# Window attention and two dense layers: the 64-token tiles of two batches as one unit

## Chip, core and metric

One core of a Trainium2 chip. The metric is the device time of one execution in microseconds (us).

## What is computed

Causal attention with a window of 128 keys and a linear bias per head (4 batches, 8 heads, 576 tokens, head dimension 64), then two dense layers in float32 on the 2304 tokens. Cut to what matters here:

```python
scores = scale * np.matmul(q, k.transpose(0, 1, 3, 2))
mask = (rel >= 0) & (rel < window)          # rel = query - key, window = 128
attn = softmax(np.where(mask, scores + bias[None], -1e9))
x = np.matmul(attn, v)                      # 4 x 8 x 576 x 64
x = x.transpose(0, 2, 1, 3).reshape(2304, 512)
x = silu(x @ w_in) @ w_out                  # 512 -> 2048 -> 512
out = relu(x @ w2_in) ** 2 @ w2_out
```

## The kernel before, in words

A sequence of 576 tokens is four tiles of 128 tokens and one tile of 64. The 16 full tiles of the four batches make four blocks of 512 columns; the four 64-token tiles make a fifth block of 256 columns. A **unit** is one tile and one pair of heads (`units`, L85): 64 units of full tiles, and 16 **narrow** units, 80 in all.

Attention of the first 20 units runs ahead of all else. The other 60 are laid between the matmuls of the first dense layer, whose `mm1(n)` (L544) is called once in each of 64 **slots** n: 12 matmuls of 512 columns, 16 slots to a block. Eight more slots (L547 to L558) do the fifth block. Units are handled in groups of four, a group to every four slots; the table `visits` (L1019 to L1031) says in which slot a group has its scores, its transposes and its values. For the group whose first unit is u = n0 + n, scores come in slot n, transposes of the probabilities in slot n + 3, and the values (probabilities times v) in slot n + 7; where the next group is narrow, values come one slot earlier, so that in those slots there are only values, and in the next only transposes. The narrow groups have their scores in slots 44, 48, 52 and 56, their transposes in 47, 51, 55 and 59, and their values in 50, 54, 58 and 63; the values of the last full group are in slot 46.

The work of a unit: `scores` (L223) multiplies 64 queries of one head by 192 keys, once for each 64 queries and each of the two heads; the head decides which half of the array's rows is used, the half of the queries decides which columns. `maxima`, `exponentials`, `reciprocals` and `normalise` are the softmax, on VectorE, ScalarE, VectorE and GpSimd. `transpose_p` (L320) turns 64 rows of probabilities at a time, `copy_p` brings them back from PSUM, `values` (L367) or `values_of_four` (L351, for narrow groups) multiplies them by v. A narrow unit has only the first half of the queries, so half as many scores and transposes as a full one; its values have 64 columns in place of 128.

Inputs come by the DMA queue of SyncE (SP), in program order with the stores of the first layer's results (`g0d`): `load_qk` and `load_v` (L202, L210) bring q, k and v of one unit four units ahead, into places of their own, four of each. The float64 weights come as words into a place of `raw` (one place, L896) or into a spare place of the pool `w` (16 places, `spare`, L404), and are turned into float32 pairs in five steps whose slots `begin` sets (L857 to L862). The last of them, chunk (0, 1, 7), begins in slot 51 and uses `raw`.

The order of the instructions is written out by hand (`manual_schedule`): every engine runs its own in program order.

Of the kernel before, what the change touches and what calls it, by code (L numbers as in the profile page):

```python
# [8 lines left out]
F32 = mybir.dt.float32  # L9
# [7 lines left out]
P = 128  # L17
# [8 lines left out]
def kernel(  # L26
# [21 lines left out]
    nc = tc.nc  # L48
    B, NHP, S, _ = v.shape
    NT, DM = out.shape  # L50
    NF = w1.shape[0]
    D = 64
# [4 lines left out]
    raw_p = ctx.enter_context(tc.tile_pool(name="raw", bufs=1))  # L57
# [13 lines left out]
    full = [(b, t, P, min(t, P)) for b in range(B) for t in range(0, S - P + 1, P)]  # L71
    rest = [(b, S // P * P, S % P, P) for b in range(B)]
    blocks = [full[i:i + NSUB] for i in range(0, len(full), NSUB)]
    blocks.append(rest)
    NB = len(blocks)
    width = [sum(t[2] for t in tiles) for tiles in blocks]
    start = [sum(width[:j]) for j in range(NB)]
    assert sum(width) == NT and max(width) <= BLK and P % rest[0][2] == 0
    tbs = []
    for j, tiles in enumerate(blocks):  # L80
        c0 = 0
        for t in tiles:
            tbs.append((j, c0) + t)
            c0 += t[2]
    units = [t + (hp,) for t in tbs for hp in range(NHP)]  # L85
    NU = len(units)
    x_t = {}

# [6 lines left out]
    def attention(ap, ps, n0):  # L95
        slope = [2.0 ** (-8.0 * (h + 1) / H) for h in range(H)]
        xq, xk, xv, z_t, s_t, pt_t, o_t = ({} for _ in range(7))
        c = {"n0": n0}

        W = 3 * D

        def halves_of(u):

            n, m0 = units[u][4:6]
            if m0 == P:
                return [(slice(0, n), slice(0, W))]
            if u < c["n0"] and not m0:
                return [(slice(0, n), slice(D, W))]  # L110
            return [(slice(i * D, (i + 1) * D), slice(P - m0 - i * D, W)) for i in range(n // D)]

        def whole(u):

            n, m0 = units[u][4:6]
            return slice(0, n), slice(D + P - m0 - (n - D if m0 < P else 0), D + W)

        def zeros(z):
            nc.gpsimd.memset(z[..., :D], 0.0)
            nc.gpsimd.memset(z[..., D + W:], 0.0)  # L120

# [70 lines left out]
        def load_v_strip(i):  # L192
# [6 lines left out]
            for hp in range(NHP):  # L199
                xv[i * NHP + hp] = [c["va"][:, i - 1, hp] if m0 else None, c["va"][:, i, hp]]  # L200

        def load_qk(u):  # L202
            _, _, b, t0, n, m0, hp = units[u]
            if u not in xq:
                xq[u] = ap.tile([P, P], F32, tag="q", name="q", bufs=4)
                nc.sync.dma_start(out=xq[u][:, :n], in_=q[b, hp, :, t0:t0 + n])
            xk[u] = ap.tile([P, 2 * P], F32, tag="k", name="k", bufs=4)[:, P - m0:P + n]
            nc.sync.dma_start(out=xk[u], in_=k[b, hp, :, t0 - m0:t0 + n])

        def load_v(u):  # L210
            _, _, b, t0, n, m0, hp = units[u]
            t = ap.tile([P, 2, P], F32, tag="v", name="v", bufs=4)
            if m0 == n:
                nc.sync.dma_start(
                    out=t, in_=v[b, hp, t0 - m0:t0 + n, :].rearrange("(k p) d -> p k d", p=P)
                )
            else:
                if m0:
                    nc.sync.dma_start(out=t[:m0, 0], in_=v[b, hp, t0 - m0:t0, :])
                nc.sync.dma_start(out=t[:n, 1], in_=v[b, hp, t0:t0 + n, :])  # L220
            xv[u] = [t[:, 0], t[:, 1]]

        def scores(u):  # L223


            _, _, b, t0, n, m0, hp = units[u]
            lo = P - m0
            xq_, xk_ = xq.pop(u), xk.pop(u)
            apart = len(xq_.shape) == 3
            if apart:  # L230
                s = acc_p.tile([P, 2, 2 * P], F32, tag="acc", name="s")
                s = [s[:, j] for j in range(2)]
            else:
                so = c["pp" if u >= c["n0"] and u % 4 > 1 else "so"]
                s = [so[:, j, u % 2 * 2 * P:(u % 2 + 1) * 2 * P] for j in range(2)]
            if u < c["n0"] and not m0:
                for j in range(2):
                    nc.tensor.matmul(
                        s[j][:D, D:P], lhsT=c["far"], rhs=c["ident"][:, :D], start=True, stop=True
                    )  # L240
            for i in range(n // D):
                for j in range(2):
                    r = slice(i * D, (i + 1) * D)
                    first = max(lo - i * D, 0)
                    keys = slice(first + i * D - lo, W + i * D - lo)
                    h = slice(0, P) if apart else slice(j * D, (j + 1) * D)
                    nc.tensor.matmul(  # L247
                        s[j][r, first:W], lhsT=xq_[:, j, r] if apart else xq_[h, r], rhs=xk_[h, keys],
                        start=True, stop=True,
                    )  # L250
            s_t[u] = s
# [96 lines left out]
                copy(to[:n, :, 1::2], pp[:n, :, 1::2])  # L348
            pt_t[u] = pt

        def values_of_four(u):  # L351

            *_, n, m0, _ = units[u]
            pts, vts = [[t.pop(u + i) for i in range(4)] for t in (pt_t, xv)]
            o = c["o"]
            for i in range(4):
                o_t[u + i] = o[:, i - i % 2:i - i % 2 + 2]
            for kb, m in ((0, m0), (1, n)):
                for i in range(4):
                    for j in range(2):  # L360
                        nc.tensor.matmul(  # L361
                            o[j * D:(j + 1) * D, i, :n], lhsT=vts[i][kb][:m, j * D:(j + 1) * D],
                            rhs=pts[i][:m, j, kb, :n], start=kb == i == 0, stop=kb == 1,
                            skip_group_check=True,
                        )

        def values(u):  # L367
            _, _, b, t0, n, m0, hp = units[u]
            pt, vt = pt_t.pop(u), xv.pop(u)
            if u % 2 == 0:  # L370
                o = c["o"]
                if u < c["n0"] - 4 and u % 4:
                    o = c.pop("late", None) or acc_p.tile([P, 4, P], F32, tag="acc", name="o")
                first = u % 4 if u >= c["n0"] - 4 else 0
                o_t[u] = o[:, first:first + 2]
            o = o_t[u - u % 2][:, u % 2]
            for kb, m in ((0, m0), (1, n)):
                if m:
                    for j in range(2):
                        nc.tensor.matmul(  # L380
                            o[j * D:(j + 1) * D, :n], lhsT=vt[kb][:m, j * D:(j + 1) * D],
                            rhs=pt[:m, j, kb, :n], start=kb == 0 or not m0, stop=kb == 1,
                        )
# [9 lines left out]
        def x_lo(u):  # L393
            xh, xl, o = halves_of_x(u)
            nc.vector.tensor_tensor(xl, o, xh.bitcast(F32), ALU.subtract)

        return (zeros, lambda: c["z"], wake, constants, biases, load_q_apart, load_k_strip, load_v_strip, load_qk, load_v, scores, maxima, exponentials,
                reciprocals, normalise, transpose_p, copy_p, values, values_of_four, x_hi, x_lo)

# [4 lines left out]
    def spare(dtype):  # L404

        return wp.tile([P, 16 * P], F32R, tag="w", name="spare").bitcast(dtype)
# [450 lines left out]
    begin = {}  # L857
    for i in range(NI):
        begin[0, 0, i] = 2 * i - 4
        begin[0, 1, i] = 2 * NI + 5 * i  # L860
    converted = [(0, 0, i) for i in range(EARLY + 1)]
    begin[0, 0, EARLY + 1] = 1  # L862

# [35 lines left out]
    with tc.manual_schedule():  # L899
# [4 lines left out]
        n0 = ends(0) + 4  # L904
        with tc.tile_pool(name="at", bufs=2) as ap, tc.tile_pool(
            name="ps", bufs=1, space=bass.MemoryType.PSUM
        ) as ps:
            (zeros, at_z, wake, constants, biases, load_q_apart, load_k_strip, load_v_strip, load_qk, load_v, scores, maxima, exponentials,
             reciprocals, normalise, transpose_p, copy_p, values, values_of_four, x_hi, x_lo) = attention(ap, ps, n0)
            assert [t[1:4] for t in blocks[0]] == [(i * P, P, min(i, 1) * P) for i in range(NSUB)]  # L910
            load_k_strip(0, slice(0, 1))
            load_q_apart(0)
# [100 lines left out]
            def some(*us):  # L1013
                return [u for u in us if u < NU]
# [4 lines left out]
            visits = {n: [(), (), ()] for n in range((NB - 1) * NF)}  # L1019
            for n in range(4, (NB - 1) * NF, 4):  # L1020
                u = n0 + n
                narrow = u < NU and units[u][4] < P
                visits[n][2] = some(*range(u, u + 4))
                visits[n + 2 if narrow else n + 3][0] = some(*range(u - 4, u))
                visits[n + 3][1] = some(*range(u, u + 4))
            u = n0
            visits[1] = (), (u - 2, u - 1), ()
# [8 lines left out]
            left = []  # L1036
            for n in range((NB - 1) * NF):
                old, mid, new = visits[n]
                if len(old) == 4 and units[old[0]][4] < P:
                    values_of_four(old[0])  # L1040
                else:
                    for u in old:
                        values(u)
                for u in mid:
                    transpose_p(u)
                for u in new:
# [51 lines left out]
        with tc.tile_pool(name="gp", bufs=1) as gp_, tc.tile_pool(  # L1098
            name="acc2", bufs=4, space=bass.MemoryType.PSUM
# [29 lines left out]
            for i in range(4):  # L1129
                n = 4 + 10 * i  # L1130
# [9 lines left out]
            for j, x in enumerate(((1, 1, 3), (1, 1, 4))):  # L1140
                n = 18 + 10 * j
# [5 lines left out]
            for i in range(5, NI):  # L1147
                n = (29, 42, 57)[i - 5]
# [23 lines left out]
            for s in range(1, 4):  # L1172
                c = 7 * 4 * s - 21
# [57 lines left out]
            for n in range(NS):  # L1231
# [6 lines left out]
                b, fs = slots[n]  # L1238
# [22 lines left out]
            for c in range(4 * NI // 2):  # L1261
                s = 2 * c // NI
# [108 lines left out]
```

## Time and profile before

| | us |
|---|---|
| median of three runs | 869.44 (869.16 to 869.87) |
| the profiled execution, its own time | 868.8 |
| its span, first to last instruction | 867.0 |
| TensorE matmul busy | 858.0 (99%) |
| TensorE weight load busy | 764.0 (88%) |
| VectorE, ScalarE, GpSimd busy | 595.9, 461.9, 139.0 |
| granted TensorE clock, mean | 1.000 of full |

The profile is one execution. Its own time is 1.8 us over its span and 0.64 us under the median. Times in the trace are from the span's start. A busy engine is not yet one that sets the end: for that the chain of waits is read, which follows back from the last instruction what released each.

### The profile page before, as it was taken

What the parts mean: (1) busy time and instruction counts of PE and PEld (TensorE: products, weight loads), DVE (VectorE), ACT (ScalarE), POOL (GpSimd) and SP (SyncE); (2) the same over time, 40 slices, a digit from 0 to 9 for tenths busy, and PEclk for the clock granted to TensorE, in tenths of its full rate; (3) what the DMA queues carried; (4) which work ended last, traced back from release to release, by engine and by line L of the source; (5) the groups of instructions that cost most, each with busy time, mean ns of one, the idle gap of its engine ahead of it and who ended that gap; (6) DMA issues with size and microseconds to landing.
All of it is one profiled execution on the core that took longest, in us unless ns stands there. A gap on an engine that the chain in (4) does not pass through costs nothing.

```text
span 867.0 us, 17373 instructions
## 1 busy us (share of the span) xinstructions
PE 858.0 (99%) x6344; PEld 764.0 (88%) x6344; DVE 595.9 (69%) x1291; ACT 461.9 (53%) x1010; POOL 139.0 (16%) x222
## 2 busy tenths in 40 slices
PE   8999999999999999999999999999999999999998
PEld 6777888878778888888888899999999999999998
DVE  6878665656552465998646546677467789899884
ACT  8778666666563443555333456556467743434331
POOL 7788433524431000000000000000000000000000
PEclk9999999999999999999999999999999999999999
DMA  9676756766542377799875454565457954444431
GB/s 273 203 220 207 213 186 192 225 212 188 164 139 102 114 256 257 253 349 352 279 274 193 146 179 160 195 248 194 165 199 292 357 171 146 147 130 139 145 102 47
DMA packets 114613, 173.64 MB, mean 200 GB/s; under 512 B 12256, under 2 KB 73952, under 8 KB 111968
## 3 DMA queue, kind: packets, MB, share of 16 engines
q1 hardware_dynamic: 114256, 172.40, 59.8%
q8 instruction: 50, 0.82, 0.4%
q14 instruction: 35, 0.29, 0.1%
q10 hardware_dynamic: 272, 0.13, 0.1%
HBM read 111.15 MB, written 61.34 MB: 199 GB/s over the span
## 4 chain that ended last, share of the span: by engine, by line
PE 97%; ACT 1%; POOL 1%; DMA 0%; DVE 0%; issue 0%; SPq 0%; DVEq 0%; POOLq 0%; ACTq 0%
PE acc L631 23%; PE acc L790 21%; PE h L564 20%; PE a L692 12%; PE d L692 6%; PE b L692 3%; PE o L380 3%; PE h L553 3%; PE so L247 1%; PE pp L331 1%; PE s L247 1%; PE pp L247 1%; PE so L331 1%; PE o L361 1%; POOL z L300 0%; DMA spare<-in_q_dram 0%
## 5 line engine op out<-in xcount | busy, mean ns | idle before, releaser
L631 PE MATMUL acc<-g,w 128*128 128x512 f32 (+1 forms) x896 | 196.9, 382 | 0.0
L631 PEld LDWEIGHTS acc<-g,w 128*128 128x128 f32 x896 | 163.7, 188 | 33.0
L564 PE MATMUL h<-x,w 128*128 128x512 f32 x768 | 185.8, 396 | 0.0
L790 PE MATMUL acc<-w,g 128*128 128x256 f32 x1512 | 181.7, 283 | 0.0
L790 PEld LDWEIGHTS acc<-w,g 128*128 128x128 f32 x1512 | 181.6, 192 | 0.0
L564 PEld LDWEIGHTS h<-x,w 128*128 128x128 f32 x768 | 141.2, 188 | 34.7 <-DVE st L273 2.8
L692 PE MATMUL a<-x,w 128*128 128x288 f32 x720 | 104.0, 295 | 0.0
L692 PEld LDWEIGHTS a<-x,w 128*128 128x128 f32 x720 | 98.6, 188 | 0.2 <-DVE ev L841 0.2
L611 ACT CAST g<-l 128x512 fp32r<-128x512 f32 x72 | 44.9, 624 | 98.5 <-PE acc L631 82.5
L612 DVE TENSOR_TENSOR g<-l,g 128x512 fp32r<-128x512 f32 x72 | 49.7, 690 | 54.5 <-ACT g L611 54.2
L300 POOL TENSOR_SCALAR z<-z,st 128x192 f32<-128x192 f32 (+2 forms) x120 | 62.7, 541 | 107.7 <-DVE st L294 78.2
L587 DVE SCALAR_TENSOR_TENSOR t<-t,h 128x512 f32<-128x512 f32 x64 | 43.7, 683 | 46.0 <-ACT t L582 45.9
L582 ACT ACTIVATE t<-h 128x512 f32<-128x512 f32 x64 | 38.1, 596 | 53.8 <-PE h L564 51.0
L283 ACT ACTIVATE z<-z,st 128x192 f32<-128x192 f32 (+2 forms) x120 | 52.5, 441 | 14.1 <-DVE st L273 13.9
L759 ACT CAST g<-l 128x1024 fp32r<-128x1024 f32 x25 | 26.3, 1050 | 61.3 <-issue 31.0
L692 PE MATMUL d<-x,w 128*128 128x288 f32 x384 | 56.4, 295 | 0.0
L692 PEld LDWEIGHTS d<-x,w 128*128 128x128 f32 x384 | 52.9, 188 | 0.0
L273 DVE CUSTOM_DVE_ANT_0 z<-so,bias 128x192 f32<-128x192 f32 (+2 forms) x68 | 19.5, 328 | 31.7 <-PE so L247 28.0
L453 POOL TENSOR_TENSOR w<-spare,w 128x512 fp32r<-128x512 f32 x24 | 36.9, 1556 | 5.6 <-ACT w L448 5.6
L1290 DVE TENSOR_TENSOR ev<-a,ev 128x288 f32<-128x288 f32 x32 | 14.1, 455 | 32.6 <-PE a L692 31.9
L766 DVE TENSOR_TENSOR g<-l,g 128x1024 fp32r<-128x1024 f32 x25 | 30.6, 1225 | 8.3 <-ACT g L759 8.3
L523 DVE TENSOR_TENSOR w<-raw,w 128x1024 fp32r<-128x1024 f32 (+1 forms) x22 | 23.7, 1087 | 10.1 <-ACT w L518 10.1
(165 smaller groups left out, 1162.0 us busy)
## 6 DMA issues: line engine op xcount, KB each, us to landing
g0d<-t SPq DMA_DIRECT2D x72, 256.0 KB, 2.7
l<-g0d SPq DMA_DIRECT2D x72, 256.0 KB, 4.9
raw<-in_w_dram SPq DMA_DIRECT2D x28, 512.0 KB, 5.4
g1d<-t SPq DMA_DIRECT2D x48, 288.0 KB, 2.4
l<-g1d SPq DMA_DIRECT2D x50, 256.0 KB, 3.3
spare<-in_w_dram SPq DMA_DIRECT2D x12, 1024.0 KB, 7.9
wd<-raw SPq DMA_DIRECT2D x10, 1024.0 KB, 4.7
raw<-wd SPq DMA_DIRECT2D x7, 1024.0 KB, 5.7
```

Of the source, the lines that this page charges most:

```text
L283: nc.scalar.activation(z[r, j, k], z[r, j, k], AF.Exp, bias=least[r, j:j + 1], scale=-1.0, accum_out=total[r, j:j + 1],)
L300: nc.gpsimd.tensor_scalar(z[r, j, k], z[r, j, k], share[r, j:j + 1], 1.0, ALU.mult, ALU.mult)
L453: nc.gpsimd.tensor_tensor(w[:, 1, a], words(x)[1][:, a].bitcast(F32), w[:, 0, a].bitcast(F32), ALU.subtract)
L564: nc.tensor.matmul(h[:, j * w:(j + 1) * w], lhsT=wi[:, wh, c * P:(c + 1) * P], rhs=x[:, xh, c, :w], start=c == 0 and i == 0, stop=c == KC ...
L582: nc.scalar.activation(t_t[n], h_t[n], AF.Tanh, scale=0.5)
L587: nc.vector.scalar_tensor_tensor(t, t, 1.0, h, ALU.add, ALU.mult)
L611: nc.scalar.copy(g[:, 0], t)
L612: nc.vector.tensor_tensor(g[:, 1], t, g[:, 0].bitcast(F32), ALU.subtract)
L631: nc.tensor.matmul(to, lhsT=wo[:, a, c * P:(c + 1) * P], rhs=g[:, z, j * w:(j + 1) * w], start=f == 0 and i == 0, stop=f == NF - 1 and i = ...
L692: nc.tensor.matmul(acc[to], lhsT=w[wh][:, c * P:(c + 1) * P], rhs=o[:, xh, c], start=r in (0, 1, 3) and c == 0 and k == 0, stop=c == 1 and ...
L766: tt(g[1][:, :, :4], a, g[0][:, :, :4].bitcast(F32), ALU.subtract)
L790: nc.tensor.matmul(acc[to][:, half], lhsT=g[x], rhs=w[y], start=i == 0 and half == 0 and j == 0, stop=i == NI - 1 and j == 2, skip_group_c ...
```

## The change

The four 64-token tiles no longer make 16 units with 64 queries each. Two batches make one **double** unit: 128 queries, of which the first 64 belong to one batch and the others to the next. There are 8 double units, two groups of four, and 72 units in all. Their probabilities lie as those of a full tile; since the two halves have different keys and values, scores take the keys of their half (`xk_[i]`), and values take their half's v and probabilities (`values_of_double` in place of `values_of_four`). In v, the 64 rows that belong to no key of the half are zero.

The queries and keys of a whole group are loaded at once into one spare place of the weights' pool `w`, the values of a group at once into `raw`; the two groups use the same places one after the other. The last chunk of weights, which also uses `raw`, begins eight slots later, in slot 59. The special slot for values before narrow groups is gone.

```diff
-    units = [t + (hp,) for t in tbs for hp in range(NHP)]
+    units = [t + (hp,) for t in tbs[:len(full)] for hp in range(NHP)]
+    twos = [t[:4] + (P, P) for t in tbs[len(full)::2]]
+    units += [t + (hp,) for t in twos for hp in range(NHP)]
...
+        def load_double_qk(u):
+            _, _, b, t0, _, _, hp = units[u]
+            if hp == 0:
+                if "qks" not in c:
+                    t = spare(F32)
+                    c["qks"] = [
+                        t[:, x:x + 2 * NHP * w].rearrange("p (h b c) -> p b h c", h=NHP, b=2)
+                        for x, w in ((0, D), (2 * NHP * D, W))
+                    ]
+                for to, x, t in zip(c["qks"], (q, k), (t0, t0 - P)):
+                    for i in range(2):
+                        nc.sync.dma_start(
+                            out=to[:, i], in_=x[b + i, :, :, t:t0 + D].rearrange("h p c -> p h c")
+                        )
+            xq[u] = c["qks"][0][:, :, hp].rearrange("p b c -> p (b c)")
+            xk[u] = [c["qks"][1][:, i, hp] for i in range(2)]
+
+        def load_double_v(u):
+            _, _, b, t0, _, _, hp = units[u]
+            if hp == 0:
+                if "vs" not in c:
+                    t = raw_p.tile([P, 16 * P], F32, tag="raw", name="vs")
+                    c["vs"] = t.rearrange("p (h i k d) -> p i k h d", h=NHP, i=2, k=2)
+                    nc.gpsimd.memset(c["vs"][D:, 0, 1], 0.0)
+                    nc.gpsimd.memset(c["vs"][:D, 1, 0], 0.0)
+                for i, kb, r, t in (
+                    (0, 0, slice(0, P), t0 - P), (0, 1, slice(0, D), t0),
+                    (1, 0, slice(D, P), t0 - P), (1, 1, slice(0, P), t0 - D),
+                ):
+                    nc.sync.dma_start(
+                        out=c["vs"][r, i, kb],
+                        in_=v[b + i, :, t:t + r.stop - r.start, :].rearrange("h p d -> p h d"),
+                    )
+            xv[u] = c["vs"][:, :, :, hp]
...
+            if not double(u):
+                xk_ = [xk_[..., max(i * D - lo, 0):W + i * D - lo] for i in range(n // D)]
...
-                    keys = slice(first + i * D - lo, W + i * D - lo)
...
-                        s[j][r, first:W], lhsT=xq_[:, j, r] if apart else xq_[h, r], rhs=xk_[h, keys],
+                        s[j][r, first:W], lhsT=xq_[:, j, r] if apart else xq_[h, r], rhs=xk_[i][h],
...
-        def values_of_four(u):
...
+        def values_of_double(u, o):
+            pt, vt = pt_t.pop(u), xv.pop(u)
+            for kb in range(2):
+                for i in range(2):
                     for j in range(2):
+                        h, r = (slice(x * D, (x + 1) * D) for x in (j, i))
                         nc.tensor.matmul(
+                            o[h, r], lhsT=vt[:, i, kb, h], rhs=pt[:, j, kb, r],
+                            start=kb == i == 0, stop=kb == 1, skip_group_check=True,
                         )
...
-        begin[0, 1, i] = 2 * NI + 5 * i
+        begin[0, 1, i] = 2 * NI + 5 * i + (i == 7) * 8
...
-                narrow = u < NU and units[u][4] < P
                 visits[n][2] = some(*range(u, u + 4))
-                visits[n + 2 if narrow else n + 3][0] = some(*range(u - 4, u))
+                visits[n + 3][0] = some(*range(u - 4, u))
                 visits[n + 3][1] = some(*range(u, u + 4))
```

On TensorE, from the scores of slot 48 on, the program before reads as follows (`so` and `pp` are PSUM places, L247 scores, L564 the first layer, L361 values of a narrow group, L331 transposes):

```order
L247 MATMUL so<-k,q 64x192 x4
L247 MATMUL pp<-k,q 64x192 x4
L564 MATMUL h<-x,w 128x512 x24
L361 MATMUL o<-pt,v 64x64 x16
L564 MATMUL h<-x,w 128x512 x12
L331 MATMUL so<-ident,z 128x64
L331 MATMUL so<-ident,z 64x64
```

The last two rows stand four times, and four times more for `pp`; then come 12 matmuls of the first layer and the next narrow group. In the changed program the same place, from slot 48 to the fifth block, reads (L296 scores, L610 the first layer, L406 values of a double group, L380 transposes):

```order
L296 MATMUL so<-spare 64x192 x8
L296 MATMUL pp<-spare 64x192 x8
L610 MATMUL h<-x,w 128x512 x36
L406 MATMUL o<-pt,vs 64x64 x32
L380 MATMUL so<-ident,z 128x64 x16
L380 MATMUL pp<-ident,z 128x64 x16
L610 MATMUL h<-x,w 128x512 x48
L406 MATMUL o<-pt,vs 64x64 x32
L610 MATMUL h<-x,w 128x512 x108
```

Half as many groups have twice as many scores, transposes and values each; from slot 44 on attention stands between the first layer's matmuls at 5 places, where it stood at 13.

On SP's queue, from the scores of slot 48 on, the program before has for each narrow group rows like these (`g0d` stores of the first layer, L414 the words of chunk (0, 1, 7)):

```order
L206 DMA q<-in_q_dram 128x64
L208 DMA k<-in_k_dram 128x192
L414 DMA raw<-in_w_dram 128x2x1024
L592 DMA g0d<-t 128x512 x2
L219 DMA v<-in_v_dram 128x128
L220 DMA v<-in_v_dram 64x128
```

The pairs of q and k and of v stand four times each. The changed program has, from the second load of queries and keys in slot 44 to the words of chunk (0, 1, 7):

```order
L221 DMA spare<-in_q_dram 128x4x64 x2
L221 DMA spare<-in_k_dram 128x4x192 x2
L638 DMA g0d<-t 128x512 x3
L240 DMA vs<-in_v_dram 128x4x128
L240 DMA vs<-in_v_dram 64x4x128 x2
L240 DMA vs<-in_v_dram 128x4x128
L638 DMA g0d<-t 128x512 x4
L240 DMA vs<-in_v_dram 128x4x128
L240 DMA vs<-in_v_dram 64x4x128 x2
L240 DMA vs<-in_v_dram 128x4x128
L638 DMA g0d<-t 128x512 x5
L460 DMA raw<-in_w_dram 128x2x1024
```

Sixteen loads stand where 64 were, each of a group and not of a unit, and the last words come after the second load of values.

## Rows read from the trace of the kernel before

**Rows 1.** The page: busy time by engine; shares of the chain that ended last.

```profile
PE 858.0 (99%) x6344; PEld 764.0 (88%) x6344; DVE 595.9 (69%) x1291; ACT 461.9 (53%) x1010; POOL 139.0 (16%) x222
...
PE 97%; ACT 1%; POOL 1%; DMA 0%; DVE 0%; issue 0%; SPq 0%; DVEq 0%; POOLq 0%; ACTq 0%
```

**Rows 2.** Busy time by stage, slots 44 to 63: length, engines, clock, DMA share, GB/s.

```profile
core 0: us, PE busy (x) PEld busy (x) DVE busy (x) ACT busy (x) POOL busy (x), PEclk, DMA share, GB/s
...
208.57:283.02 74.45, 74.45 (x529) 58.39 (x529) 33.88 (x116) 39.31 (x131) 22.25 (x38) 1.00 0.44 145
```

**Rows 3.** Chain of waits, slots 44 to 63: start, length, engine, tile, line, count.

```profile
208.64 0.80 PE so L247 x8
209.44 0.65 PE pp L247 x8
210.09 5.71 PE h L564 x24
215.79 1.90 PE o L380 x32
217.69 2.94 PE h L564 x12
220.63 0.61 PE so L331 x8
221.24 0.47 PE pp L331 x8
221.71 2.96 PE h L564 x12
...
231.82 1.23 PE o L361 x32
233.05 2.97 PE h L564 x12
...
267.87 11.12 PE h L564 x48
278.99 1.23 PE o L361 x32
280.22 2.97 PE h L564 x12
283.19 22.60 PE h L553 x128
```

**Rows 4.** Chain of waits, the last full groups, slots 35 to 43.

```profile
171.80 1.02 PE o L380 x16
...
192.77 0.81 PE so L247 x16
193.58 0.65 PE pp L247 x16
194.23 8.43 PE h L564 x36
...
204.56 0.64 PE so L331 x16
205.20 0.50 PE pp L331 x16
```

**Rows 5.** Timeline, first half of one narrow group's values; line L361, 128-row form.

```profile
231.75 0.69 PE L361 MATMUL o<-pt,v 128*64 128x64 f32 x16
...
L361 PE MATMUL o<-pt,v 128*64 128x64 f32 x64 | 2.7, 228 | 0.0
```

**Rows 6.** DMA: one load of words near slot 43; all landings into `spare`.

```profile
spare<-in_w_dram SPq DMA_DIRECT2D x1, 1024.0 KB, 8.1
...
DMA to landing us min/median/max: 1.9/5.2/11.5
```

**Rows 7.** GpSimd: timeline near slot 46; memsets of 64 by 512.

```profile
217.33 2.57 POOL L453 TENSOR_TENSOR w<-raw,w 128x512 fp32r<-128x512 f32 x2
...
L171 POOL MEMSET spare<- 64x512 f32 x2 | 1.0, 520 | 0.1
```

More of the change, by code (lines that the diff above doesn't have):

```diff
@@ L84 @@
             c0 += t[2]
-    units = [t + (hp,) for t in tbs for hp in range(NHP)]
+    units = [t + (hp,) for t in tbs[:len(full)] for hp in range(NHP)]
+    twos = [t[:4] + (P, P) for t in tbs[len(full)::2]]
+    assert rest[0][2] == P // 2 and len(rest) % 2 == 0
+    units += [t + (hp,) for t in twos for hp in range(NHP)]
     NU = len(units)
@@ L102, in attention, with double @@
         W = 3 * D
+        def double(u):
+            return units[u][0] == NB - 1
         def halves_of(u):
@@ L200, in load_v_strip @@
                 xv[i * NHP + hp] = [c["va"][:, i - 1, hp] if m0 else None, c["va"][:, i, hp]]
+        def load_double_qk(u):
[31 more added lines that the diff above has]
+            xv[u] = c["vs"][:, :, :, hp]
         def load_qk(u):
+            if double(u):
+                return load_double_qk(u)
             _, _, b, t0, n, m0, hp = units[u]
@@ L210, in load_v @@
         def load_v(u):
+            if double(u):
+                return load_double_v(u)
             _, _, b, t0, n, m0, hp = units[u]
@@ L349, in copy_p @@
             pt_t[u] = pt
-        def values_of_four(u):
[L353 to L359, printed above, removed]
+        def values_of_double(u, o):
+            pt, vt = pt_t.pop(u), xv.pop(u)
+            for kb in range(2):
+                for i in range(2):
                     for j in range(2):
+                        h, r = (slice(x * D, (x + 1) * D) for x in (j, i))
                         nc.tensor.matmul(
-                            o[j * D:(j + 1) * D, i, :n], lhsT=vts[i][kb][:m, j * D:(j + 1) * D],
-                            rhs=pts[i][:m, j, kb, :n], start=kb == i == 0, stop=kb == 1,
-                            skip_group_check=True,
+                            o[h, r], lhsT=vt[:, i, kb, h], rhs=pt[:, j, kb, r],
+                            start=kb == i == 0, stop=kb == 1, skip_group_check=True,
                         )
@@ L368, in values @@
             _, _, b, t0, n, m0, hp = units[u]
-            pt, vt = pt_t.pop(u), xv.pop(u)
             if u % 2 == 0:
@@ L376, in values @@
             o = o_t[u - u % 2][:, u % 2]
+            if double(u):
+                return values_of_double(u, o)
+            pt, vt = pt_t.pop(u), xv.pop(u)
             for kb, m in ((0, m0), (1, n)):
@@ L397, in attention @@
         return (zeros, lambda: c["z"], wake, constants, biases, load_q_apart, load_k_strip, load_v_strip, load_qk, load_v, scores, maxima, exponentials,
-                reciprocals, normalise, transpose_p, copy_p, values, values_of_four, x_hi, x_lo)
+                reciprocals, normalise, transpose_p, copy_p, values, x_hi, x_lo)
     w_t, raw_t = {}, {}
@@ L908 @@
             (zeros, at_z, wake, constants, biases, load_q_apart, load_k_strip, load_v_strip, load_qk, load_v, scores, maxima, exponentials,
-             reciprocals, normalise, transpose_p, copy_p, values, values_of_four, x_hi, x_lo) = attention(ap, ps, n0)
+             reciprocals, normalise, transpose_p, copy_p, values, x_hi, x_lo) = attention(ap, ps, n0)
             assert [t[1:4] for t in blocks[0]] == [(i * P, P, min(i, 1) * P) for i in range(NSUB)]
@@ L1038 @@
                 old, mid, new = visits[n]
[L1039 to L1043, printed above, removed]
+                for u in old:
+                    values(u)
                 for u in mid:
```

## The prediction

> **What bounds the kernel now.** I read the page first. TensorE is busy 99% of the span, and the chain that ended last runs through TensorE for 97% of it [rows 1]. So time is won or lost only where TensorE's own stream gets shorter or where it has to wait. Second, the busy times of the stretch that the change touches, from the scores of slot 44 to the fifth block's first matmul: TensorE is busy for all of its 74.45 us at the full clock (1.00, the 2.4 GHz level), VectorE for 33.88, ScalarE for 39.31, GpSimd for 22.25, and the DMA engines for 44% [rows 2]. Nothing but TensorE is near its limit there. Third, the chain in order of time, which cuts that stretch into pieces of TensorE's stream [rows 3] and gives the pieces of a full group just ahead of it [rows 4]. These are the prices. The chain's clock puts the stretch at 208.64 to 283.19, which is 74.55 us.
>
> The trace records each matmul of scores and of values twice, and transposes and the first layer's once: the program's x4 of a narrow score row are x8 in the chain. My counts are of records.
>
> **The change on TensorE.** No matmul is taken away. The scores stay 64 records of 192 columns, the transposes 64, the narrow values 128 records of 64 columns. What changes is how they stand together. The stretch now holds 20 slots of the first layer and:
>
> *Scores.* A narrow group takes 0.80 + 0.65 = 1.45 us for 16 records; four groups, 5.80 [rows 3]. A full group takes 0.81 + 0.65 = 1.46 us for 32 [rows 4]. The second half of the queries, which writes the other half of the columns, costs 0.01 us. A double group has the matmuls of a full group in shape, count and order, so I take 1.46, and 2.92 for two. Won: 2.88 us.
>
> *Transposes.* A narrow group takes 0.61 + 0.47 = 1.08 us for 16; four, 4.32 [rows 3]. A full group takes 0.64 + 0.50 = 1.14 for 32, alternating between the upper and the lower half of the rows [rows 4]. A double group does the same: 2.28 for two. Won: 2.04 us.
>
> *Values.* A narrow group takes 1.23 us for 32 records; four, 4.92 [rows 3]. A double group has 64 records of 64 columns, with all 128 rows as weights, and the trace has no such group. From below: 32 records of 128 columns, the same number of columns, take 1.90 [rows 3]. From above: two narrow groups, 2.46. I choose between them by the first half of a narrow group, which has 128 rows too: 16 records last 0.69 us, of which 0.23 is the last one's own length, so they start within 0.46, 58 ns to a pair of heads [rows 5]. The two halves of a narrow group are 16 pairs, 0.93 us; the other 0.30 of its 1.23 is going over to 128 rows and, half way, to 64 rows, some 0.15 each. A double group is 32 pairs with one such step: 32 x 0.058 + 0.15 = 2.01 us, near the lower end. Two groups: 4.02. Won: 0.90 us, between 0.0 and 1.12.
>
> *The first layer.* 12 matmuls standing alone take 2.94 to 2.97 us, 24 take 5.71, 36 take 8.43, 48 take 11.12 [rows 3, 4]: 2.72 for each slot, and 0.24 for each time that the stream comes back from attention. Before, attention stood at 13 places in the stretch: four scores, five values, four transposes, all apart. After, it stands at five: the scores of slots 44 and 48, values with transposes behind them in 47 and 51, and the values of slot 55. Eight steps fewer: won 8 x 0.24 = 1.92 us. That values and transposes side by side cost nothing extra is seen in the full groups, where the transposes behind values take 1.14 for twice the number [rows 4].
>
> The sum is 2.88 + 2.04 + 0.90 + 1.92 = 7.7 us. The other way round: 55.6 for 20 slots in five runs (8.43 + 2.94 + 8.43 + 11.12 + 24.7), 2.92 scores, 2.28 transposes, 1.90 for the last full values and 4.02 make 66.7, and 74.55 - 66.7 = 7.8.
>
> **What else moves, and what hides it.** On VectorE, ScalarE and GpSimd the softmax of eight units goes away, and the copies change shape. That is hidden, and costs or gives nothing: these engines have 35 to 52 us free in the stretch [rows 2]. In slots 44 to 51 they do for a double group what they did every four slots before, without holding TensorE.
>
> The DMAs: 64 loads become 16 with the same bytes, so SP issues less. The second load of queries and keys overwrites the place that the scores of slot 44 read, so it starts when they end, at 210.1, and the scores of slot 48 need it after 8.43 + 1.90 + 1.14 + 2.94 = 14.4 us. It is 1 MB. The nearest row, a load of 1 MB of words, lands in 8.1 us, and the slowest landing in any spare place is 11.5 [rows 6]; about 2 us go to the four issues. So it is hidden with 1 to 4 us to spare. Behind it in SP's queue stand only the stores of the first layer, which are due slots later.
>
> The values of slot 51 go into `raw`, which chunk (0, 1, 5) leaves when GpSimd's two subtractions end at 217.33 + 2.57 = 219.9 [rows 7]. Then come two memsets of 0.52 each [rows 7], and the load can go at 221. The values need it at 234. SP stands at that load from slot 47 on, with the stores of slots 45 and later behind it; their places are written again four slots on, so a stand of 3 us is hidden.
>
> The words of chunk (0, 1, 7) now come in slot 56 and are turned over in slots 59 to 63, where there is no softmax left. The second layer's matmuls come to them last of the chunks. The extra place in `w` is given back when the scores of slot 48 are done, and the next cast into it, that of chunk (0, 1, 6), is in slot 49 and needs it just then: it comes after work of ScalarE that needs those scores itself, so there is no new wait.
>
> Later stages run by the same slots and start 7.7 us earlier, with their loads.
>
> **The forecast.** The sum is made against the profiled execution, 868.8 us, which is 0.64 under the median of the three runs. 869.44 - 7.7 = **861.7 us**. With the ends for the values it is 861.4 to 862.6; the three runs of the kernel before lie 0.7 apart, so I let the low end go to 860.9.
>
> **The rivals.**
>
> *The halves don't overlap.* If the scores and transposes of the second batch's half stood behind those of the first, each double group would cost two narrow ones. Then 2.88 + 2.04 of the gain go: 866.6. It speaks for it that the keys of the two halves now come from two places, where a full tile reads one; against it that the full groups have the same shapes in the same order at 1.46 and 1.14 [rows 4]. Chance 4%.
>
> *The weight loads of the values stand in line.* All of them fill the same 128 rows. The nearest row where loads of the same rows follow each other is a narrow group's transposes, all in the upper half: 1.08 / 16 = 68 ns for each [rows 3]. At that pace 64 records take 4.3 us, 2.3 more than I took, and two groups 4.6: 866.3. Against it: the first half of a narrow group's values has 128 rows and takes 43 ns per record with its start and end [rows 5], and 32 records of full values take 59 ns each for twice the columns [rows 3]. Chance 4%. The Trainium skill has this rule, in "TensorE: Matmul & The Clock Gate", Part 3, What overlaps and what doesn't: a weight load overlaps with running matmuls only where the row groups differ. By that rule this case holds; the trace does not agree, with 58 ns for a pair of records on the same rows.
>
> *Slower: the second load of queries and keys comes late.* TensorE would stand at the scores of slot 48, and each us past 14.4 us after the scores of slot 44 is lost. The gain is used up at 14.4 + 7.7 = 22 us, and the kernel is measurably slower from 24 on. At 27 us it would be 874. For it: it is 1 MB in pieces of 256 and 768 bytes, behind 1 MB of words. Against it: the slowest landing in a spare place is 11.5 us [rows 6]. Chance of slower 3%, of a loss that eats most of the gain 2%.
>
> *The time is given back later.* Some later load or conversion doesn't come 7.7 us earlier, TensorE waits for it, and the time stays at 869.4. For it: `raw` is in use eight slots longer before the second layer's words want it. Against it: chunk (0, 1, 7) leaves it as the fifth block begins, and the next load into it comes after the fifth block's 22.60 us [rows 3]. Chance 3%.
>
> **How the numbers follow.** The forecast has 84%. The predicted time is its 861.7. The range goes from 860.9 to 864.5, which takes in the bounds of the values, the spread of the runs, and the two overlap rivals where they come true by half; what it leaves out are these in full and the last two. About what a measurement of this kernel can tell from no change is 0.2%, 1.7 us. Faster by more than that: forecast and both overlap rivals, 92%. Within: 5% (the time given back, and the late load in part). Slower: 3%.
>
> **What would show it.** In the changed kernel's chain: scores with x16 at 0.8 and 0.65 us twice; values of 64 records at 2.0 (2.3 or more would say that the upper end was right, 4 that the loads stand in line); transposes of 32 at 1.14; five returns to the first layer, the last run of 108 taking 24.7; the fifth block's first matmul near 275.4. No wait of TensorE on a DMA at slots 48, 51 or 55. If the fifth block begins at 275.4 and the end does not come 7.7 us earlier, a later stage gave it back. The forecast is wrong if the scores of a double group take over 2 us, or if TensorE shows a wait in that stretch.

## The result, and the profile after

The changed kernel takes **861.64 us** (median of five runs, 860.75 to 862.62) against 869.16 for the kernel before in the same comparison (five runs, 868.75 to 869.87): a ratio of 0.9911, with a 95% interval of 0.9900 to 0.9922. That is 7.5 us faster. The forecast was 861.7, with a range of 860.9 to 864.5.

The page of the changed kernel, busy time by engine and the chain's shares, which answer to [rows 1]:

```profile
PE 850.2 (99%) x6344; PEld 760.6 (88%) x6344; DVE 590.0 (69%) x1247; ACT 451.9 (52%) x950; POOL 132.5 (15%) x208
...
PE 93%; DMA 2%; SPq 1%; DVE 1%; issue 1%; ACT 1%; POOL 1%; DVEq 0%; ACTq 0%; POOLq 0%
```

TensorE has the same 6344 instructions and is busy 7.8 us less. It is still what sets the end; the few per cent that the chain now runs through DMA and SP lie in the first 20 us and at one store near 152 us, ahead of the change.

The chain in order of time, from the scores of slot 44 to the fifth block, answers to [rows 3] (columns as there; L296 scores, L610 the first layer, L426 values of full units, L406 values of double units, L380 transposes, L599 the fifth block):

```profile
209.50 0.81 PE so L296 x16
210.31 0.65 PE pp L296 x16
210.96 8.43 PE h L610 x36
219.38 1.90 PE o L426 x32
221.28 0.65 PE so L380 x16
221.93 0.51 PE pp L380 x16
222.43 2.94 PE h L610 x12
225.38 0.81 PE so L296 x16
226.19 0.65 PE pp L296 x16
226.84 8.38 PE h L610 x36
235.22 2.02 PE o L406 x64
237.24 0.64 PE so L380 x16
237.88 0.51 PE pp L380 x16
238.38 11.10 PE h L610 x48
249.49 2.02 PE o L406 x64
251.50 24.71 PE h L610 x108
276.21 22.60 PE h L599 x128
```

This is the whole stretch, piece by piece as forecast. It runs from 209.50 to 276.21, 66.71 us, where it took 74.55 before [rows 3]: 7.84 us less. Between its pieces TensorE never waits.

The busy times of that stretch answer to [rows 2]:

```profile
208.60:275.30 66.70, 66.70 (x529) 54.70 (x529) 28.50 (x72) 30.28 (x71) 17.40 (x24) 1.00 0.45 153
```

TensorE has the same number of records in it (529) and is busy throughout, at the full clock. VectorE has 5.4 us less to do, ScalarE 9.0, GpSimd 4.9. (The window lies 0.9 us ahead of this kernel's stretch; over 209.50 to 276.20 the busy times of these three are the same.)

In the profiled executions the spans differ by 6.2 us (867.0 and 860.8), not by 7.84. The stretch begins 0.86 us later in the changed kernel's execution, after a start in which the instructions are the same, and the part behind the fifth block is some 0.8 longer. Over all the executions profiled for this study the first piece behind the start, the values that begin at 35.61 us in the kernel before, begins anywhere from 35.1 to 37.2 us. The medians carry this scatter; the stretch does not. So below each experiment is read in the stretch first and in the median second.

### The profile page after: what moved, and what is told of

It is laid out like the page before. It is cut to its first block, busy times and chain, and to the rows that moved or that the text cites. A ratio compares the mean times of both kernels' runs of the same rounds, so it can differ in the third digit from the quotient of the medians.

```text
span 860.8 us, 17142 instructions
## 1 busy us (share of the span) xinstructions
PE 850.2 (99%) x6344; PEld 760.6 (88%) x6344; DVE 590.0 (69%) x1247; ACT 451.9 (52%) x950; POOL 132.5 (15%) x208
## 4 chain that ended last, share of the span: by engine, by line
PE 93%; DMA 2%; SPq 1%; DVE 1%; issue 1%; ACT 1%; POOL 1%; DVEq 0%; ACTq 0%; POOLq 0%
PE acc L677 23%; PE acc L836 20%; PE h L610 19%; PE a L738 12%; PE d L738 6%; PE b L738 3%; PE o L426 3%; PE h L599 3%; PE so L296 1%; PE pp L380 1%; DMA g0d<-t 1%; DMA spare<-in_w_dram 1%; PE pp L296 1%; PE so L380 1%; SPq L181 1%
## 5 line engine op out<-in xcount | busy, mean ns | idle before, releaser
L610 PE MATMUL h<-x,w 128*128 128x512 f32 x768 | 183.1, 394 | 0.0
L610 PEld LDWEIGHTS h<-x,w 128*128 128x128 f32 x768 | 141.8, 188 | 33.6 <-DVE st L322 1.9
L349 POOL TENSOR_SCALAR z<-z,st 128x192 f32<-128x192 f32 (+1 forms) x104 | 55.2, 553 | 87.6 <-DVE st L343 50.6
L332 ACT ACTIVATE z<-z,st 128x192 f32<-128x192 f32 (+1 forms) x104 | 45.3, 437 | 13.4 <-DVE st L322 13.2
L322 DVE CUSTOM_DVE_ANT_0 z<-so,bias 128x192 f32<-128x192 f32 (+2 forms) x60 | 17.1, 327 | 26.3 <-PE so L296 22.6
```

Of the source, the lines that this page charges most:

```text
L332: nc.scalar.activation(z[r, j, k], z[r, j, k], AF.Exp, bias=least[r, j:j + 1], scale=-1.0, accum_out=total[r, j:j + 1],)
L349: nc.gpsimd.tensor_scalar(z[r, j, k], z[r, j, k], share[r, j:j + 1], 1.0, ALU.mult, ALU.mult)
L610: nc.tensor.matmul(h[:, j * w:(j + 1) * w], lhsT=wi[:, wh, c * P:(c + 1) * P], rhs=x[:, xh, c, :w], start=c == 0 and i == 0, stop=c == KC ...
```

## The experiments

Each kernel was compared with the kernel before on the same chip. Its medians were 869.31 for the first four runs, 869.74 for the next four, and 869.50 for the last two. "Stretch" is the time from the scores of slot 44 to the fifth block: 74.55 us before, 66.71 in the changed kernel.

### e1: the returns alone, in the kernel before

```diff
-                visits[n + 2 if narrow else n + 3][0] = some(*range(u - 4, u))
+                visits[n + 3][0] = some(*range(u - 4, u))
```

> The kernel before, with one part of the change alone: the values of the last full group and of the narrow groups stand in the slot of the transposes, so that attention stands at 9 places from slot 44 on and no longer at 13. Theory (each return to the first layer's matmuls costs 0.24 us, whatever stands there): 4 returns fewer, 1.0 us faster, 868.2 us against 869.2; in the chain a single narrow group's values stay at 1.23, its transposes at 1.08, and the runs of 12 matmuls in slots 46 and 47 become one run of 36 before them, as in the full groups. Rival (the returns cost nothing by themselves, and all of the gain is in doubling the groups): 869.2.

Measured: 868.18 us, a ratio of 0.9982 (0.9969 to 0.9995). One narrow group in the chain:

```profile
226.60 8.43 PE h L564 x36
235.03 1.23 PE o L361 x32
236.25 0.61 PE so L331 x8
236.87 0.47 PE pp L331 x8
237.33 2.96 PE h L564 x12
```

Values and transposes keep their prices when they stand side by side, 1.23 and 1.08. Three slots of the first layer run as 8.43, where 5.71 and 2.97 stood [rows 3], 0.25 more. The stretch goes from 209.35 to 282.93, 73.58 us: 0.97 less for four returns. The theory holds, and the rival is out.

### e5: two returns given back, in the changed kernel

```diff
-                visits[n + 3][0] = some(*range(u - 4, u))
+                visits[n + 2 if 44 <= n <= 48 else n + 3][0] = some(*range(u - 4, u))
```

> The changed kernel, with the values of the last full group in slot 46 and those of the first double group in slot 50, apart from the transposes in 47 and 51, as the kernel before had them: attention stands at 7 places from slot 44 on instead of 5. Theory (each return to the first layer costs 0.24 us): 2 x 0.24 = 0.5 us slower than the changed kernel, 862.1, and in the chain the 20 slots of the first layer take 55.6 + 0.5 = 56.1 us; values 1.90 and 2.02, scores 1.46, transposes stay at 1.08 to 1.14. Rival (the returns are not what the first layer's pieces gained): the pieces add up to 55.6 again.

Measured: 861.78 us, a ratio of 0.9906 (0.9888 to 0.9924), which the median cannot tell from the changed kernel. The stretch can: 208.90 to 276.02, 67.12 us, 0.41 more for two returns, 0.2 each. The first layer's pieces add up to 55.94 against 55.56. The price of a return is confirmed in sign and roughly in size.

### e2: scores and transposes by halves

The four units' matmuls of the first batch's half come first, then those of the second batch's half; nothing is added or left out.

```diff
+        def scores_by_halves(us):
...
+            for i in range(2):
+                for u in us:
+                    for j in range(2):
+                        r, h = (slice(x * D, (x + 1) * D) for x in (i, j))
+                        nc.tensor.matmul(
+                            s_t[u][j][r, :W], lhsT=xq[u][h, r], rhs=xk[u][i][h], start=True, stop=True
+                        )
...
+        def transposes_by_halves(us):
+            for i in range(2):
+                for u in us:
+                    for j in range(2):
+                        for kb in range(2):
...
```

> The changed kernel, with the same scores and transposes of the two double groups in another order: first those of the first batch's half for all four units, then those of the other half. Theory (the second half is nearly free because its matmuls stand next to those of the first half and run beside them in the other half of the columns or rows): a double group's scores go from 1.46 to about 2.7 to 2.9 us, its transposes from 1.14 to about 2.1; 2 x 2.2 to 2 x 2.4 = 4.4 to 4.8 us slower than the changed kernel, about 866.2. Rival (a group's scores and transposes have mostly a fixed price, whatever their number and order): scores 1.46, transposes 1.14, 861.6.

Measured: 864.97 us, a ratio of 0.9951 (0.9936 to 0.9966), 3.3 slower than the changed kernel. The first double group's scores in the chain, and the first layer behind them:

```profile
208.13 0.80 PE so L279 x8
208.93 0.16 PE pp L279 x2
209.09 0.07 PE so L279 x2
209.16 0.10 PE pp L279 x2
209.25 0.07 PE so L279 x2
...
209.58 0.06 PE so L279 x2
209.64 0.65 PE pp L279 x8
210.29 8.38 PE h L640 x36
```

They take 208.13 to 210.29, 2.16 us, not 1.46. The transposes of a group, 1.96 (220.57 to 222.53), not 1.15. The stretch is 208.13 to 277.82, 69.69 us: 2.98 more, which is 2 x 0.70 and 2 x 0.81. So the order matters, and the rival, a fixed price in any order, is out. But the price is 3.0 us and not the 4.4 to 4.8 expected, and the rows above say why: even in this order the halves are not wholly apart. The program has `so` x8 and `pp` x8 of the first half, then the same of the second; in the chain the second half's first records on `so` start between the first half's last on `pp`.

The starts in the traces, read record by record, give the price. In a narrow group of the kernel before, records start two at a time: at 0 and 6 ns from the group's first, then at 213 and 220, at 375 and 382, and so on every 163 ns to 1188 and 1195. These are eight rounds. In a double group of the changed kernel four start in each round (0, 6, 13 and 20 ns in the first), and the eight rounds come at the same times. That is why 32 records take what 16 took: eight rounds are 1.30 us, and only some 0.16 of the 1.46 is for the ends. In e2 two records start in each round until the second half sets in, 0.71 us after the first, when six of the first half's 16 have yet to start; then the two halves share four rounds. That makes 12 rounds, 1.95 us, and the ends. Halves wholly apart would take 16 rounds, 2.76 us with the ends; this is an estimate, no run shows it, and it is what I had expected.

Transposes behave alike: one starts every 58 ns in a narrow group, two within 4 ns of each other every 62 ns in a double one. In e2 one starts at a time, until the second half sets in with three of the first half's still to start.

### e10: scores by heads

```diff
-            for i in range(2):
-                for u in us:
-                    for j in range(2):
+            for j in range(2):
+                for u in us:
+                    for i in range(2):
```

This is the order of e2 with the head outermost, for the scores alone; the transposes are the changed kernel's.

> The changed kernel, with the scores alone of the double groups in another order: first those of one head (the upper rows) for all units, left and right columns in turn, then those of the other head. Theory (a group needs neighbours in all four quarters of the array; with two only, the price is that of the order by halves, whichever two they are): 2.16 us a group in place of 1.46, 2 x 0.70 = 1.4 us slower than the changed kernel, 863.0. Rival (only the columns must alternate, rows do not matter): 1.46, 861.6.

Measured: 864.22 us, a ratio of 0.9936 (0.9922 to 0.9951). The scores take 2.17 and 2.16 us (210.28 to 212.45, 226.88 to 229.04), and the stretch 68.20, 1.49 more. Here too the second head's first records start 0.71 us after the first head's. Two kinds of neighbours give the same price whether they differ in rows or in columns; for 1.46 records of all four kinds have to start in one round.

### e8: the four kinds crosswise

```diff
-            for i in range(n // D):
-                for j in range(2):
+            for i, j in ((0, 0), (1, 1), (0, 1), (1, 0)):
```

> The changed kernel, with the four kinds of matmul of a unit's scores in another order in every unit: upper rows to left columns, then lower rows to right columns, then the two others, so that neighbours share neither rows nor columns. Theory (all four run beside each other in either order): scores stay at 1.46 a group, 861.6. Rival (neighbours that share columns still hold each other up): scores get shorter, by up to a third of 1.46 in each of some 13 groups, up to 6 us faster.

Measured: 861.93 us, a ratio of 0.9910 (0.9893 to 0.9928). Scores stay at 0.81 + 0.65 in both double groups and in the full groups just ahead of them, and the stretch is 208.64 to 275.40, 66.76. With all four kinds in turn, these two orders cost the same.

### e3: values by heads

```diff
-            for kb in range(2):
-                for i in range(2):
-                    for j in range(2):
+            for j in range(2):
+                for kb in range(2):
+                    for i in range(2):
```

> The changed kernel, with the values of a double unit ordered by heads: the four matmuls of one head, then the four of the other. Theory (the two heads run beside each other, each in its half of the columns, so a pair takes 58 ns): with the heads apart each record takes about 58 ns alone, a double group's 64 records go from 2.0 to about 3.6 us, 2 x 1.6 = 3.2 us slower than the changed kernel, about 864.8. Rival (each record takes 29 ns by itself, the pace of issuing them or of loading weights): values stay at 2.0, 861.6.

Measured: 864.01 us, a ratio of 0.9944 (0.9926 to 0.9963). The chain:

```profile
235.38 2.62 PE o L406 x64
...
250.25 2.62 PE o L406 x64
```

The values of a group take 2.62 us, neither 2.0 nor 3.6. The stretch is 209.66 to 277.58, 67.92: 1.21 more, twice 0.60. The starts in the trace say why. Records of one head start 58 ns apart, as the theory has it; but the other head's first record starts 0.29 us after this head's first, when three of this head's eight are still to start, and the two heads then run beside each other for a while. So it goes at every change of head: of 64 records, 21 start within 7 ns of one before them, where in the changed kernel 32 do. That leaves 43 steps of 58 ns in place of 32; with 0.15 for the ends 2.64 us and 2.01, against 2.62 and 2.02 measured. So a pair does take 58 ns, and the 3.6 expected was for heads wholly apart, which this order does not give. The rival is out too. The median is 2.4 over the changed kernel's, more than the stretch shows; the rest is in the scatter of the start and the end, which four runs do not settle.

### e4: the second load comes late

```diff
                 for u in new:
-                    if u + 4 < NU:
+                    if u + 4 < NU and n != 44:
                         load_qk(u + 4)
...
                 store_t(n - 2)
+                if n == 47:
+                    for u in range(NU - 4, NU):
+                        load_qk(u)
```

> The changed kernel, with the second load of queries and keys moved in SP's queue from slot 44 to behind the load of values of slot 47 and one store. Theory (the load is hidden in the changed kernel with some 5 us to spare, and each us beyond is lost one for one): SP comes to it at 225.2 us in that kernel's trace, its four issues take 2.1 and it lands 6.5 us later, near 233.8, while the scores of slot 48 want it at 225.4: TensorE stands for about 8.4 us, the gain is gone, about 870 us. Rival (the loads have so much room that 14 us less does nothing, or TensorE gets the time back in later slots): 861.6.

Measured: 871.19 us, a ratio of 1.0027 (1.0016 to 1.0039): slower than the kernel before. The chain at slot 48:

```profile
221.67 2.96 PE h L610 x12
...
226.37 5.42 DMA spare<-in_k_dram
...
231.83 1.23 PE so L296 x10
```

The last of the keys land at 231.8, and TensorE's longest wait in this run is for the keys:

```profile
PE so L296 <- DMA spare<-in_k_dram: 6.2, 1, 6.2
```

So the rival of the prediction that ends slower is a real mechanism: a late load is paid for. In the changed kernel SP issues this load from 210.98 to 213.1, and a piece of it lands 6.5 us after its issue (median of the two loads of keys), near 219.6, while the scores begin at 225.4: some 6 us of cover. Busy time and clock by stage, the last three columns being the granted clock, the DMA share and GB/s:

```profile
208.70:230.80 22.10, 15.91 (x145) 12.76 (x144) 9.22 (x28) 11.23 (x29) 8.25 (x12) 0.93 0.57 179
230.80:234.60 3.80, 3.68 (x33) 2.10 (x33) 1.04 (x7) 0.64 (x3) 0.00 (x0) 0.50 0.15 55
```

TensorE stood for 6.2 us, until 230.8, and the scores that followed ran at a granted clock of 0.50, the 1.2 GHz level; the next two us are at 1.00 again. From the wait's end to the first layer they took 3.8 us in place of 1.46: about 1 us until the last keys were there, and from then 2.8 us at half the clock. The stretch from 208.73 to 284.06 is 75.33 us, 8.6 more than the changed kernel's: 6.2 for the wait and 2.4 for scores that came in two parts and at half the clock. I had expected 8.4 of standing alone; the keys landed 2 us earlier than that, and the clock made up most of the difference, so that the total of 8.6 came near mine by luck. The first layer behind them takes what it takes in the changed kernel, so nothing is got back.

### e6: the late words alone, in the kernel before

```diff
-        begin[0, 1, i] = 2 * NI + 5 * i
+        begin[0, 1, i] = 2 * NI + 5 * i + (i == 7) * 8
```

> The kernel before, with one part of the change alone: the last chunk of weights, (0, 1, 7), is loaded and turned over eight slots later, in slots 59 to 63. Theory (its work on VectorE, ScalarE and GpSimd is hidden wherever it stands, and TensorE comes to these weights much later): 869.2 us, no change beyond 0.2%, the stretch from slot 44 to the fifth block stays at 74.5. Rival (the shift itself gives or costs something, since it takes the conversion out of the softmax or puts it next to the fifth block): a change of over 0.5 us in that stretch or a wait of TensorE in the fifth block.

Measured: 869.56 us, a ratio of 1.0003 (0.9994 to 1.0013). The stretch is 209.29 to 283.84, 74.55, and the chain's pieces there are those of the kernel before. The shift is free by itself.

### e7 and e9: the softmax work given back

```diff
+        def softmax_again(u):
+            so = c["pp" if u % 4 > 1 else "so"]
+            s_t[u] = [so[:, j, u % 2 * 2 * P:(u % 2 + 1) * 2 * P] for j in range(2)]
+            maxima(u)
+            exponentials(u)
+            if u % 2:
+                reciprocals(u)
+                normalise(u - 1)
+                normalise(u)
...
+                if 56 <= n < 60:
+                    for u in range(NU - 8 + 2 * (n - 56), NU - 6 + 2 * (n - 56)):
+                        shared["softmax_again"](u)
```

> The changed kernel, with the softmax work that fell away given back to VectorE, ScalarE and GpSimd: in slots 56 to 59 eight units' maxima, exponentials, reciprocals and normalising run once more on places that nobody reads any more. Theory (that work was hidden behind TensorE and its removal gave nothing): no change, 861.6 us, and the run of 108 matmuls stays at 24.7. Rival (part of the gain came from relieving these engines): up to 8 x 0.8 = 6 us slower, with waits of TensorE on VectorE in slots 56 to 63.

Measured in e7: 862.88 us, a ratio of 0.9926 (0.9909 to 0.9942). My expectation missed. The run of 108 matmuls takes 25.84 instead of 24.7 (250.65 to 276.49), and TensorE waits once in slots 44 to 63:

```profile
PE h L622 <- DVE t L645: 0.8, 1, 0.8
```

The chain from slot 56 on shows why (L640 and L645 are the two steps of the first layer's activation, L322 and L332 the added maxima and exponentials):

```profile
253.63 0.61 ACT t L640
254.26 0.69 DVE t L645
254.95 0.27 DVE z L322
255.26 0.86 ACT z L332 x3
256.16 0.97 ACT z L332 x4
257.13 0.49 ACT t L640
```

One round from activation to activation is 3.5 us, where a slot is 2.72. It goes over VectorE and back to ScalarE, so it adds up though neither engine is full. Three such rounds, 253.63 to 263.95, fall 2.2 us behind. The fourth, to 269.50, takes 5.55, and 2.2 of that are two steps of the last words' conversion on VectorE (L488, 0.84, and L489, 1.32). Together they fall 5 us behind, more than the three PSUM places of the first layer hold off. e9 spreads the same work over eight slots:

```diff
-                if 56 <= n < 60:
-                    for u in range(NU - 8 + 2 * (n - 56), NU - 6 + 2 * (n - 56)):
-                        shared["softmax_again"](u)
+                if 52 <= n < 60:
+                    shared["softmax_again"](NU - 8 + n - 52)
```

> The changed kernel, with the same softmax work of eight units given back as in the run that put it into four slots, but spread: one unit in each of slots 52 to 59. Theory (the work is hidden as long as its chain from ScalarE over VectorE and back fits into a slot's 2.72 us, which one unit's half of the 3.4 us chain does and two units' did not): 861.6 us, no wait of TensorE in slots 52 to 63, the run of 108 matmuls at 24.7. Rival (this work always costs TensorE something, and its removal was part of the gain): the run of 108 grows by over 0.5 us again, 862.2 or more.

Measured in e9: 862.52 us, a ratio of 0.9919 (0.9902 to 0.9935). The run of 108 is back at 24.71, the stretch at 66.72, and TensorE waits nowhere in it. The median lies 0.9 over the changed kernel's, but the intervals overlap, and the stretch shows nothing to put it down to. In that stretch VectorE, ScalarE and GpSimd are busy for 34.34, 37.91 and 23.97 us, about as much as before the change [rows 2]. So the work was hidden, as forecast, and its removal gave nothing; it is hidden as long as its chain fits into a slot.

## Why the prediction was right

By its own steps, in the chain of the changed kernel:

| step | forecast, us | measured, us |
|---|---|---|
| scores of two double groups | 2.92 | 2.92 |
| transposes of two | 2.28 | 2.31 |
| values of two | 4.02 | 4.04 |
| last full group's values | 1.90 | 1.90 |
| first layer, 20 slots in five runs | 55.6 | 55.56 |
| the stretch | 66.7 | 66.71 |

*What bounds the kernel.* TensorE did, and the 7.84 us that its stream lost in this stretch came out at the end as 7.5, within what the medians can tell: the interval of the ratio reaches from 6.8 to 8.7 us. That the median lands 0.06 from the forecast is luck. From the fifth block's start to the end of the span the profiled executions take 583.8 to 584.3 us with narrow groups (three kernels) and 584.1 to 584.8 with double ones (nine), so a few tenths may be given back there; the scatter is as large.

*Scores and transposes.* The price was read off the full groups [rows 4], and it held to 0.03 us. The starts show the reason: the second half's records start in the same rounds as the first half's. e2 and e10 change only the matmuls' order, so that fewer start in one round, and the price rises.

*Values.* The choice near the lower bound was right (2.02 against 2.01). The reading behind it, 58 ns to a pair that runs side by side and 0.15 for the ends, is what the starts of the records show, in the changed kernel and in e3. The low end of 861.4 does not quite follow from its own sum, which gives 861.5.

*Returns.* Forecast 0.24 each; e1 shows 0.24 for four in one kernel, e5 0.2 for two in the other. All eight together, with the pieces of the first layer at 57.66 us before and 55.56 after, gave 2.10 and not the 1.92 forecast. This accounts for the difference between the 7.7 of the first sum and the 7.84 of the stretch.

*What was hidden.* The other engines' work (e9), the late words (e6) and the loads (no wait in the stretch) cost nothing. The second load of queries and keys had more room than I gave it, about 6 us and not 1 to 4: I took 8.1 us for its landing, from a load of words, and its pieces land in 5.8 to 6.5. The load of values went a little later than 221, at 222.25, since GpSimd's two subtractions took 4.00 us and not 2.57, and it was as harmless.

*The rivals.* The overlap rival is refuted by the starts and by 2.92 and 2.31. With one half's matmuls behind the other's in the program it would have cost 3.0 us and not 4.9, since TensorE starts part of the second half beside the first (e2). That the weight loads of values stand in line is refuted by 2.02. The late load is real, and its price, put as one for one, leaves out the clock (e4). The time was not given back later, but for the few tenths named above at most.

## What to carry to other kernels

Where an engine is busy without a gap, price an edit by the pieces of its stream in the chain, and take the price of a new group from the nearest group of the same shape and order, not from twice the smaller one. A group of small matmuls is priced by its rounds of starts (eight rounds of 163 ns for 16 scores and for 32 here), and each return to large matmuls costs 0.2 to 0.26 us. Filling the idle half of a tile with a second batch is then nearly free for scores and transposes, if the matmuls of both halves stand in turn; the values, which keep all their columns, gained 0.44 us for each double group. Before calling two orders "together" and "apart", look at the starts: an order in the program that is meant to separate two kinds of matmul need not separate them on the engine. Loads that feed such a group need their cover measured, since a wait of TensorE here was paid once in time and again in clock.

## What the runs showed of the hardware that I had not expected

- Scores of one quarter of the array start every 163 ns, and those of the other quarters within 20 ns beside them: 32 records take 1.46 us with all four in turn, in either of two orders (e8), and 2.16 with two in turn, the same for either pair (e2, e10).
- Matmuls do not start in program order throughout: those of another quarter, or of another head's columns, start beside earlier ones while some of the earlier group have yet to start, six of 16 in e2 and three of eight in e3. What sets how far ahead they start stays open.
- Values with all 128 rows start 58 ns apart on one head's columns, and two at a time with the heads in turn, 29 ns a record (e3).
- After TensorE had stood for 6.2 us its clock was at the 1.2 GHz level for the next 3.8 us, and the last 2.8 us of them are a group's scores that otherwise take 1.46 (e4).
- The first piece behind the start begins up to 2 us earlier or later (35.1 to 37.2) in executions of programs with the same start, more than most of the single effects here; those show in the chain and not in the medians.
